# An MLP on scaled f16 pairs in place of fp32r pairs, with a range check and the old program behind it

## The chip, the core and the metric

The kernel runs on one core of a Trainium2 chip. The metric is device time in microseconds (us). TensorE (PE) multiplies matrices, VectorE (DVE) and ScalarE (ACT) work on elements, GpSimd (POOL) takes a few small things, SyncE (SP) issues the DMAs. The profile shows one execution, and its times count from the first instruction.

## The reference

```python
scores = (q @ k.T) / 8 + decay, causal            # 4 batches, 8 heads, 576 tokens, head size 64
x = softmax(scores) @ v                           # then as 2304 tokens x 512
h = x @ moe_w_in;   g = relu(h) ** 2;  x2 = g @ moe_w_out           # 512 -> 2048 -> 512
h = x2 @ moe2_w_in
g = where(h >= 1, h, where(h <= -1, 0, (h + 1) ** 2 / 4))
out = g @ moe2_w_out
```

q, k, v and f (from which the decay is a cumulated logarithm) are float32, the four weights float64. All but moe2_w_out are drawn eight times larger than the plain draw.

## The kernel before

The output is computed transposed, features on the partitions, tokens along the free dimension. The 2304 tokens are cut into four blocks: 0, 1 and 2 of 512 tokens, and a last one of 768. For every block attention comes first and then the two MLPs (`mo` 0 and 1). The attention of a later block is spread between the MLP steps of the blocks ahead of it, so all engines have two kinds of work at the same time.

Blocks 0 to 2 go through 96 steps (3 blocks x 2 MLPs x 16 feature chunks of 128). A step does 12 matmuls of 512 columns for the hidden part (`h_group`, L1122 to L1138) and 12 for the output part (`out_group`, L1170 to L1191). They are 12 because every operand is a pair of fp32r numbers, the value rounded and the rest: upper by upper, upper by rest, rest by upper. `act_group` (L1140) does the activation on ScalarE and VectorE and makes the pair `gh`, `gl` of the result; `finish` (L1193) makes the pair of x2 or writes the output.

The weights arrive as float64. `w_load` loads them, `decode` (L1041) makes fp32 out of the bits on ScalarE, VectorE and sometimes GpSimd, `w_split` (L1092) makes the pair. All of that happens while block 0 is worked on, 32 pairs of chunks in 32 steps. The pairs go to DRAM (`scr`), and every later step loads them from there.

The last block (`last_block`, L1300) works on quarters: 384 tokens by halves of the features, with the sums of a Strassen scheme that saves matmuls: `weight_sums` and `pair_sums` (L1236, L1272) make sums of weights, `token_sums` (L1311) of tokens. Matmuls there have 384 columns and lie in L1383, L1469 to L1471 and L1517. Per MLP there are eight pairs of chunks; nine of the sixteen have a hidden part of 42 matmuls (`seven`), seven one of 48, and all have 18 + 24 of the output part: 378 + 336 + 672 in sum.

The attention has its own matmuls: L701, L744 and L758 for the first 256 tokens of a sequence, L850, L851 and L957 for the rest.

`copies` (L622) rounds an operand to its upper part, on ScalarE (L626) or VectorE (L629); `subs` (L635) subtracts, on VectorE (L638); `add` (L1228) adds on VectorE (L1230). `top` (L643) is a masked minimum that also gives out an accumulated value.

The order of all of it is made on the host before the program is written: every operation has one or more engines with an estimated cost (`mm_t`, `act_t`, `dve_t` and the like), a due time, the operations it depends on and the buffers it holds. `Schedule.improve` tries several weights and due times with a model of the engines, keeps the shortest plan, and `emit` writes the instructions in that order. Every engine then runs its instructions in order. Which engine takes an operation with a choice, and which operation goes first, can thus change in all places when one cost changes. Buffers come from rings: `big` holds six buffers of 8 KB a partition for raw float64 weights and for pairs alike.

```python
def mm_t(n):
    return (n + 32) / 2400.0
```

Of the kernel before, what the change touches and what calls it, by code (L numbers as in the profile page):

```python
# [12 lines left out]
I32 = mybir.dt.int32  # L13
# [13 lines left out]
PS = 2.0 ** 15  # L27
LAG = 2
# [330 lines left out]
def mm_t(n):  # L359
    return (n + 32) / 2400.0  # L360
# [43 lines left out]
def tile_attention_moe_moe(ctx: ExitStack, tc: tile.TileContext, qkv, f, w2, outT):  # L404
    nc = tc.nc
    PSUM = bass.MemoryType.PSUM
# [54 lines left out]
    ring("sum", 2, [P, 2, 512], F32R, late=True)  # L461
    ring("ghl", 3, [P, 2, HALF], F32R, late=True)
    ring("xa", 1, [P, NKC, 2, 512], F32R)
    ring("xb", 1, [P, NKC, 2, WIDTH[LAST]], F32R)
# [26 lines left out]
    for s in range(NS):  # L491
        g, att = s // NFC, 0.0
        for blk, (g0, g1) in ATTENTION.items():
            if g0 <= g < g1:
                att += sum(pe_time(t) for t in [*tasks, *groups] if t.blk == blk) / (NFC * (g1 - g0))
        V.append(V[-1] + 24 * mm_t(nb(s)) + att)
# [29 lines left out]
    def setup():  # L526
        sb = new("xb", "setup", [P, 2 * NKC * WIDTH[LAST]], F32)
# [9 lines left out]
        sch.op(due + 90, {"POOL": (0.05, lambda: G.memset(half, 0.5))})  # L537
# [84 lines left out]
    def copies(out, in_, n, engines="ACT DVE POOL", psum=False):  # L622

        alts = {}
        if "ACT" in engines:
            alts["ACT"] = (act_t(n, psum), lambda: nc.scalar.activation(out(), in_(), AF.Copy))  # L626
        if "DVE" in engines:
            alts["DVE"] = (
                dve_t(n) if psum else dve2_t(n), lambda: nc.vector.tensor_copy(out(), in_()), *([] if psum else [True]))  # L629
# [5 lines left out]
    def subs(out, a, b, n, engines="DVE POOL"):  # L635
        alts = {}
        if "DVE" in engines:
            alts["DVE"] = (dve_t(n), lambda: nc.vector.tensor_sub(out(), a(), b()), True)  # L638
        if "POOL" in engines:
            alts["POOL"] = (pool2_t(n), lambda: nc.gpsimd.tensor_sub(out(), a(), b()))  # L640
        return alts
# [7 lines left out]
    def attention32(g):  # L649
# [67 lines left out]
        def recips(c, st, n, deps):  # L717
            def recip():
                nc.vector.tensor_scalar(st.tile[:, 1, :n], st.tile[:, 1, :n], 1e-9, None, op0=ALU.add)
                nc.vector.reciprocal(st.tile[:, 2, :n], st.tile[:, 1, :n])  # L720
# [31 lines left out]
        def products(c, got):  # L752
# [11 lines left out]
            for kcs in ([[0], [1]] if first else [[0, 1]]):  # L764
# [7 lines left out]
            xops.setdefault((g.blk, kc), []).append(sch.op(t0 + 5.5, {  # L772
                "DVE": (dve_t(HEAD), lambda kc=kc, hi=hi, av=av: nc.vector.tensor_tensor(
                    x.tile[:, kc, 1, g.off:g.off + HEAD], av.tile[:, :HEAD], hi().bitcast(F32), op=ALU.subtract))},
                [o3], [av, x]))
# [209 lines left out]
    def split_x(blk, kcs, off, src, n, deps, buf, due):  # L985

        x, unit, m = xb[blk], 1.0 / PS, n * len(kcs)
# [5 lines left out]
        o4 = sch.op(due + 0.5, {"DVE": (dve_t(m), lambda: nc.vector.scalar_tensor_tensor(  # L993
            lo(), src(), unit, hi().bitcast(F32), op0=ALU.mult, op1=ALU.subtract), True)}, [o3], [buf, x])
# [6 lines left out]
    scr = [dram.tile([P, 2, 2, 512], F32, name=f"scr{i}") for i in range(32)]  # L1001
# [5 lines left out]
    def w_load(s):  # L1007
# [10 lines left out]
        if first:  # L1018
            b = new("big", f"raw{s}", [P, 2, 512], U64) if W64 else new("wf", f"wf{s}")
# [12 lines left out]
        if again:  # L1032
            b = whl[s] = new("big", f"whl{s}")
            for pair, layers in again.items():
                c = span(layers)
                ops.append(sch.op(V0(s + 2) - 7, {
                    "SP": (dma_t(P * 4096 * len(layers), late=1.2), lambda b=b, c=c, pair=pair: nc.sync.dma_start(
                        out=b.tile[:, c].bitcast(F32), in_=scr[pair][:, c]))},
# [53 lines left out]
    def w_split(s):  # L1092
# [6 lines left out]
        if s not in whl:  # L1099
# [4 lines left out]
        src, unit = lambda: w.tile[:, c], 2.0 if W64 else 1.0  # L1104
# [4 lines left out]
        o = sch.op(due + 1, {"DVE": (dve_t(n), lambda: nc.vector.scalar_tensor_tensor(  # L1109
            lo(), src(), unit, hi().bitcast(F32), op0=ALU.mult, op1=ALU.subtract), True)}, [o], [w, b])  # L1110
        whl_op[s].append(o)
        for pair, layers in new_pairs[s].items():
            c_ = span(layers)
            store = sch.op(due + 6, {"SP": (dma_t(P * 4096 * len(layers)), lambda c_=c_, pair=pair: nc.sync.dma_start(
                out=scr[pair][:, c_], in_=b.tile[:, c_].bitcast(F32)))}, [o], [b])
# [6 lines left out]
    def h_group(s):  # L1122
# [6 lines left out]
        for kc in range(NKC):  # L1129
# [7 lines left out]
            o = sch.op(V[s] + 0.01 * kc, {"PE": (3 * mm_t(n), mms)}, [o, *whl_op[s - LAG], *deps], [ps, w, src], mlp=True)  # L1137
        h_op[s] = (ps, o)  # L1138

    def act_group(s):  # L1140
# [8 lines left out]
        if mo == 0:  # L1149
# [6 lines left out]
            o3 = sch.op(due + 0.5, {"ACT": (act_t(n), lambda: A.activation(gh.tile[:, :n], r.tile[:, :n], AF.Square))},  # L1156
                        [o1], [r, gh])
        else:
            o1 = sch.op(due, {"ACT": (act_t(n, True, 1), lambda: A.activation(  # L1159
                r.tile[:, :n], ps(), AF.Relu, scale=0.5, bias=half))}, [o], [psb, r])  # L1160
# [3 lines left out]
                g.tile[:, :n], r.tile[:, :n], 1.0, ps(), op0=ALU.min, op1=ALU.max))}, [o1], [psb, r, g])  # L1164
            o3 = sch.op(due + 0.5, copies(lambda: gh.tile[:, :n], lambda: g.tile[:, :n], n, "ACT DVE"), [o2], [g, gh])
        o4 = sch.op(due + 1, subs(
            lambda: gl.tile[:, :n], lambda: g.tile[:, :n], lambda: gh.tile[:, :n].bitcast(F32), n, "DVE"), [o2, o3], [g, gh, gl])
        gt[s] = (gh, gl, o3, o4)

    def out_group(s, when):  # L1170
# [4 lines left out]
        for d in range(NKC):  # L1175
# [14 lines left out]
            if fc == NFC - 1:  # L1190
                finish(blk, mo, d, a, n, when)  # L1191
# [552 lines left out]
```

## Time and profile before

| | |
|---|---|
| three runs | 916.62, 918.34, 918.52 us; median 918.34 |
| profiled execution, its span | 917.6 us (its time outside the span isn't given) |
| PE busy | 906.0 us, 99%, 4620 matmuls |
| DVE busy | 819.7 us, 89% |
| ACT busy | 693.4 us, 76% |
| POOL busy | 40.9 us, 4% |
| DMA | 264 MB by queue 1, 90.9% of 16 engines |
| granted clock of PE | 0.998 on the mean |

A busy share is an average over stages with different limits. Matmuls are pipelined: the time shown for one is longer than its distance from the next. A group of instructions is a line of code, an engine and a shape, with count, busy time and mean time of one, and behind the bar the idle time of the engine ahead of it and what ended it. The chain is the work that ended last, followed back from the end.

### The profile page before, as it was taken

The page shows a single profiled execution, that of the slowest core. Times are in us where ns is not written, and L with a number is a line of the kernel's source. Part 1 is how long each engine was busy: PE and PEld are TensorE (multiplying, and loading weights), DVE is VectorE, ACT ScalarE, POOL GpSimd, SP SyncE. Part 2 cuts the span into 40 slices and gives each one's busy share as a digit, 9 for nine tenths or more (in the row PEclk, how much of TensorE's full clock was granted, in tenths as well). Part 3 has the DMA queues.
Part 4 walks back from the last instruction along what each step waited for, and adds up shares of the span by engine and source line. Part 5 has one row for each costly group of instructions (what it writes and reads, how often), then busy time and mean ns, then how long its engine had stood idle before and what let it go on. Part 6 is the DMA issues. An engine that isn't in the chain of part 4 may idle for free.

```text
span 917.6 us, 14421 instructions
## 1 busy us (share of the span) xinstructions
PE 906.0 (99%) x4620; PEld 789.0 (86%) x4620; DVE 819.7 (89%) x1888; ACT 693.4 (76%) x1391; POOL 40.9 (4%) x134
## 2 busy tenths in 40 slices
PE   7999999999999999999999999999999999999998
PEld 6778788887888888888888888888899999999998
DVE  7999999999889889988788977999798997899994
ACT  6999889899878877987787787888674455566553
POOL 4101002220000000000000000000000000000000
PEclk9999999999999999999999999999999999999999
DMA  7899999898999997999999998998888988859782
GB/s 214 243 339 418 313 404 323 327 363 306 337 339 299 305 313 221 277 309 303 253 286 286 321 301 261 229 307 230 225 283 268 334 309 286 259 186 308 265 315 86
DMA packets 139835, 264.96 MB, mean 289 GB/s; under 512 B 91120, under 2 KB 95632, under 8 KB 124976
## 3 DMA queue, kind: packets, MB, share of 16 engines
q1 hardware_dynamic: 139752, 264.04, 90.9%
q8 instruction: 37, 0.61, 0.3%
q14 instruction: 38, 0.31, 0.1%
q10 hardware_dynamic: 8, 0.00, 0.0%
HBM read 186.22 MB, written 56.80 MB: 265 GB/s over the span
## 4 chain that ended last, share of the span: by engine, by line
PE 82%; DVE 9%; ACT 4%; DMA 2%; issue 2%; POOL 1%; DVEq 0%; ACTq 0%; POOLq 0%
PE h L1132 24%; PE acc L1183 8%; PE acc L1185 8%; PE acc L1184 8%; PE h L1517 6%; PE av L957 4%; PE X L1383 3%; PE Y L1383 2%; PE s L850 2%; PE s L851 2%; PE b L1469 2%; PE b L1470 2%; PE b L1471 2%; DMA PT<-PP 1%; PE c L1469 1%
## 5 line engine op out<-in xcount | busy, mean ns | idle before, releaser
L1132 PE MATMUL h<-x,whl 128*128 128x512 f32 x1128 | 283.1, 394 | 1.3 <-DVE whl L1109 0.7
L1132 PEld LDWEIGHTS h<-x,whl 128*128 128x128 f32 x1128 | 209.5, 188 | 45.2 <-DVE whl L1109 1.6
L1183 PE MATMUL acc<-gh,whl 128*128 128x512 f32 x384 | 150.8, 393 | 0.0
L1185 PE MATMUL acc<-gl,whl 128*128 128x512 f32 x384 | 150.3, 391 | 0.0
L1184 PE MATMUL acc<-gh,whl 128*128 128x512 f32 x384 | 149.9, 390 | 0.0
L1185 PEld LDWEIGHTS acc<-gl,whl 128*128 128x128 f32 x384 | 72.1, 188 | 15.6
L1183 PEld LDWEIGHTS acc<-gh,whl 128*128 128x128 f32 x384 | 72.1, 188 | 13.7 <-issue 0.5
L884 ACT ACTIVATE E<-E,st 128x448 f32<-128x448 f32 (+2 forms) x96 | 63.6, 663 | 26.6 <-DVE st L645 20.4
L1184 PEld LDWEIGHTS acc<-gh,whl 128*128 128x128 f32 x384 | 72.2, 188 | 13.4
L638 DVE TENSOR_TENSOR gl<-g,gh 128x512 fp32r<-128x512 f32 x96 | 68.6, 714 | 5.9 <-ACT gh L626 3.9
L926 DVE SCALAR_TENSOR_TENSOR PP<-E,st,PP 128x512 f16<-128x512 f32 (+2 forms) x128 | 70.3, 594 | 3.5 <-ACT PP L922 2.8
L922 ACT ACTIVATE PP<-E,st 128x512 f16<-128x512 f32 (+2 forms) x128 | 67.3, 590 | 4.7 <-DVE st L896 4.4
L645 DVE CUSTOM_DVE_ANT_0 E<-s,mask 128x288 f32<-128x288 f32 (+2 forms) x128 | 59.5, 498 | 6.2 <-PE s L851 5.7
L626 ACT ACTIVATE pr<-PT 128x640 fp32r<-128x640 f16 (+2 forms) x69 | 36.0, 571 | 16.7 <-DMA PT<-PP 16.5
L629 DVE CAST pr<-PT 128x640 fp32r<-128x640 f16 (+2 forms) x91 | 32.7, 408 | 16.2 <-DMA PT<-PP 16.0
L957 PE MATMUL av<-pr,vt 128*128 128x320 f32 (+2 forms) x288 | 44.4, 298 | 0.0
L957 PEld LDWEIGHTS av<-pr,vt 128*128 128x128 f32 x288 | 41.6, 189 | 2.9 <-issue 0.2
L1159 ACT ACTIVATE r<-h,half 128x512 f32<-128x512 f32 x48 | 32.5, 677 | 11.9 <-PE h L1132 11.6
L1163 DVE SCALAR_TENSOR_TENSOR g<-r,h 128x512 f32<-128x512 f32 x48 | 32.7, 682 | 8.6 <-ACT r L1161 7.7
L851 PE MATMUL s<-K,Q 128*128 128x288 f32 (+2 forms) x128 | 39.6, 317 | 0.0
L850 PE MATMUL s<-K,Q 128*128 128x288 f32 (+2 forms) x128 | 39.0, 316 | 0.1
L1053 ACT ACTIVATE wf<-raw 128x1024 f32<-128x1024 f32 (+1 forms) x31 | 34.5, 1114 | 6.0 <-DVE whl L1109 6.0
(390 smaller groups left out, 1993.9 us busy)
## 6 DMA issues: line engine op xcount, KB each, us to landing
whl<-scr SPq DMA_DIRECT2D x56, 1024.0 KB
raw<-in_w_dram SPq DMA_DIRECT2D x28, 1024.0 KB
scr<-whl SPq DMA_DIRECT2D x28, 1024.0 KB
wo<-scr SPq DMA_DIRECT2D x48, 512.0 KB
in<-in_qkv_dram SPq DMA_DIRECT2D x32, 608.0 KB
wi<-scr SPq DMA_DIRECT2D x23, 512.0 KB
si<-in_sum SPq DMA_DIRECT2D x18, 512.0 KB
whl<-scr SPq DMA_DIRECT2D x16, 512.0 KB
```

The lines of the kernel that those rows point to most:

```text
L638: alts["DVE"] = (dve_t(n), lambda: nc.vector.tensor_sub(out(), a(), b()), True)
L645: return nc.vector.tensor_tensor_reduce(out=out, in0=ps, in1=mask[:m, OFF - q0:OFF - q0 + n], scale=scale, scalar=3e38, op0=ALU.add, op1=A ...
L850: nc.tensor.matmul(out, q2[:, q0:q0 + m], k2[:, s0:s1], start=True, stop=False)
L851: nc.tensor.matmul(out, Q1.tile[:, q0:q0 + m], K1.tile[:, s0:s1], start=False, stop=True)
L884: nc.scalar.activation(Ec.tile[:m, :e], Ec.tile[:m, :e], AF.Exp, scale=-1.0, bias=nmx(), accum_out=st.tile[:m, 1, ci:ci + 1])))}, [*tops, ...
L922: nc.scalar.activation(hi, x, AF.Copy, scale=r())
L926: nc.vector.scalar_tensor_tensor(lo, x, r(), hi, op0=ALU.mult, op1=ALU.subtract)
L957: nc.tensor.matmul(av.tile[:, c0:W], vt.tile[:, kc, :, :], dst()[:, i, :], start=(j == 0), stop=(j == len(parts) - 1))
L1132: nc.tensor.matmul(ps.tile[:, :n], w.tile[:, 0, wi, kc * P:(kc + 1) * P], src.tile[:, kc, xi, :n], start=(kc == 0 and i == 0), stop=(kc == ...
L1183: nc.tensor.matmul(a.tile[:, :n], wh, gh.tile[:, :n], start=(fc == 0), stop=False)
L1184: nc.tensor.matmul(a.tile[:, :n], wl, gh.tile[:, :n], start=False, stop=False)
L1185: nc.tensor.matmul(a.tile[:, :n], wh, gl.tile[:, :n], start=False, stop=(fc == NFC - 1))
```

## The change

MLP operands become f16 pairs. Weights are multiplied by 2^10, x by 2^10, x2 by 2^2, the first activation by 2^4 and the second by 1, and the scales are taken out again where results leave PSUM. The attention keeps fp32r. The function is called twice with a new argument `halves`. In the call with `halves` on, every subtraction that makes a rest of weights, x, x2, weight sums or token sums, and every instruction that makes an output, also gives out its sum along the free dimension into a column of `seen`. `out_of_range` squares and sums these columns, compares six totals with limits, and the second call, the program of before on fp32r, stands in a conditional block that runs when one of them is outside. Scratch tensors in DRAM and rings get half the bytes; `big` has seven buffers and raw weights have a ring of three of their own. Some plain subtractions and additions become `scalar_tensor_tensor`, since a scale has to go in. The planner's cost of a matmul is changed for `halves`.

```diff
+SW, SX, SG = 2.0 ** 10, (2.0 ** 10, 2.0 ** 2), (2.0 ** 4, 1.0)
+SEEN = {"w": (48, 4.0, 1e30), "x": (64, 0.25, 1e30), "x2": (32, 0.25, 1e30), "s": (64, -1.0, 1e30), "t": (32, -1.0, 1e30),
+        "o": (32, 2.0 ** 16, 1e36)}
-def mm_t(n):
-    return (n + 32) / 2400.0
+def mm_t(n, halves=False):
+    return (n + (6 if halves else 32)) / 2400.0
...
+    T, TD, NB = (F16, F16, 2) if halves else (F32R, F32, 4)
+    sw, sx, sg = (SW, SX, SG) if halves else (1.0, (1.0, 1.0), (1.0, 1.0))
+    sh = [sw * x for x in sx]
...
-    ring("big", 6, [P, 2, 2, 512], F32R)
-    ring("gh", 3, [P, 512], F32R)
-    ring("gl", 2, [P, 512], F32R)
+    ring("big", 7 if halves else 6, [P, 2, 2, 512], T)
+    if halves:
+        ring("raw", 3, [P, 2, 512], U64, early=True)
+    ring("gh", 3, [P, 512], T)
+    ring("gl", 2, [P, 512], T)
...
+    def subs(out, a, b, n, engines="DVE", psum=False, scale=1.0, seen=None):
+
+        def run():
+            if scale == 1.0 and not seen:
+                nc.vector.tensor_sub(out(), a(), b())
+            else:
+                kw = {"accum_out": seen()} if seen else {}
+                nc.vector.scalar_tensor_tensor(out(), a(), scale, b(), op0=ALU.mult, op1=ALU.subtract, **kw)
+
+        return {"DVE": (dve_t(n) + (0.06 if seen else 0.0), run, *([] if psum else [True]))}
...
-        o = sch.op(due + 1, {"DVE": (dve_t(n), lambda: nc.vector.scalar_tensor_tensor(
-            lo(), src(), unit, hi().bitcast(F32), op0=ALU.mult, op1=ALU.subtract), True)}, [o], [w, b])
+        o = sch.op(due + 1, subs(lo, src, lambda: wide(hi()), n, scale=unit, seen=mark("w")), [o], [w, b])
...
+    def result_copy(out, src, n):
+        if not halves:
+            return copies(out, src, n, "ACT DVE", psum=True)
+        to = mark("o")
+        return {"ACT": (act_t(n, True) + 0.1, lambda: nc.scalar.activation(out(), src(), AF.Copy, scale=so[1], accum_out=to()))}
...
+            def plus_old(due, out, ps, old, deps, bufs, mo=mo, seen=None):
+                kw = lambda: {"accum_out": seen()} if seen else {}
+                return sch.op(due, {"DVE": (dve_t(n) + (0.06 if seen else 0.0), lambda: nc.vector.scalar_tensor_tensor(
+                    out(), ps(), so[mo], old(), op0=ALU.mult, op1=ALU.add, **kw()))}, deps, bufs)
...
+def out_of_range(ctx: ExitStack, tc: tile.TileContext, seen, marks):
...
+    v.memset(one, 1.0)
+    for i, (kind, (m, lo, hi)) in enumerate(SEEN.items()):
+        x = seen[kind][:, :marks[kind]]
+        v.scalar_tensor_tensor(x, x, 1.0, x, op0=ALU.mult, op1=ALU.mult, accum_out=sq[:, i:i + 1])
+        v.memset(lims[:, i, 0:1], lo)
+        v.memset(lims[:, i, 1:2], hi)
+    nc.sync.dma_start(out=lim, in_=lims)
+    total, count = ps.tile([n, 1], F32, name="total"), ps.tile([1, 1], F32, name="count")
+    nc.tensor.matmul(total, sq, one, start=True, stop=True)
+    v.tensor_tensor(ok[:, 0:1], total, lim[:, 0:1], op=ALU.is_ge)
+    v.tensor_tensor(ok[:, 1:2], total, lim[:, 1:2], op=ALU.is_le)
+    v.tensor_tensor(ok[:, 0:1], ok[:, 0:1], ok[:, 1:2], op=ALU.mult)
+    nc.tensor.matmul(count, ok[:, 0:1], one[:n], start=True, stop=True)
+    v.tensor_scalar(bad, count, n - 0.5, None, op0=ALU.is_lt)
+    return nc.values_load(bad[0:1, 0:1], min_val=0, max_val=1)
...
-        tile_attention_moe_moe(tc, *args, outT)
+        with tc.tile_pool(name="seen", bufs=1) as pool:
+            seen = {kind: pool.tile([P, m], _mybir.dt.float32, name=f"seen_{kind}") for kind, (m, _, _) in SEEN.items()}
+            marks = tile_attention_moe_moe(tc, *args, outT, True, seen)
+            bad = out_of_range(tc, seen, marks)
+        with tc.If(bad > 0):
+            tile_attention_moe_moe(tc, *args, outT, False, None)
```

## Rows read from the trace of the kernel before

**Rows 1.** The page, part 1: busy us of each engine, share, instructions.
```profile
PE 906.0 (99%) x4620; PEld 789.0 (86%) x4620; DVE 819.7 (89%) x1888; ACT 693.4 (76%) x1391; POOL 40.9 (4%) x134
```
**Rows 2.** Stretches: from:to, length, busy us (count) by engine, PEclk, DMA, GB/s.
```profile
40.00:222.00 182.00, 181.21 (x859) 146.28 (x858) 173.84 (x303) 164.53 (x277) 19.85 (x14) 1.00 0.95 353
222.00:663.00 441.00, 440.26 (x2134) 371.53 (x2133) 386.03 (x978) 354.50 (x737) 8.76 (x91) 1.00 0.99 284
...
700.00:866.00 166.00, 165.13 (x939) 162.03 (x938) 153.42 (x319) 95.38 (x188) 0.00 (x0) 1.00 0.82 278
```
**Rows 3.** The chain that ended last: shares by engine, then two pieces (start, us, what).
```profile
PE 82%; DVE 9%; ACT 4%; DMA 2%; issue 2%; POOL 1%; DVEq 0%; ACTq 0%; POOLq 0%
...
596.27 2.72 PE h L1132 x12
...
793.73 7.80 PE h L1517 x45
```
**Rows 4.** Stretches again, of L1132 on PE (two rows) and of L1184 (two rows).
```profile
40.00:222.00 182.00, 91.77 (x361) 1.00 0.95 353
222.00:663.00 441.00, 195.25 (x785) 1.00 0.99 284
...
40.00:222.00 182.00, 43.68 (x112) 1.00 0.95 353
222.00:663.00 441.00, 102.70 (x264) 1.00 0.99 284
```
**Rows 5.** Groups by shape on VectorE: busy us, mean ns, idle time ahead and its end.
```profile
L926 DVE SCALAR_TENSOR_TENSOR PP<-E,st,PP 64x384 f16<-64x384 f32 x32 | 19.5, 608 | 2.6 <-ACT PP L922 2.0
L638 DVE TENSOR_TENSOR ghl<-G,ghl 128x384 fp32r<-128x384 f32 x32 | 17.7, 553 | 0.9 <-ACT ghl L626 0.2
L894 DVE TENSOR_SCALAR st<-st 128x3 f32<-128x3 f32 x32 | 5.4, 168 | 4.8 <-ACT E L884 4.0
L645 DVE DVE_READ_ACCUMULATOR2_ANT mm<- 128x1 f32 x64 | 5.2, 81 | 0.0
L814 DVE TENSOR_SCALAR Q<-in 64x320 fp32r<-64x320 f32 x10 | 3.1, 311 | 1.5 <-DMA in<-in_qkv_dram 1.5
L736 DVE TENSOR_SCALAR E1q<-E1q,st1q 128x256 f32<-128x256 f32 x4 | 1.3, 346 | 0.0
L736 DVE TENSOR_SCALAR E1q<-E1q,st1q 128x128 f32<-128x128 f32 x4 | 1.1, 280 | 0.0
```
**Rows 6.** Stretches again, of L629 on VectorE, the last block.
```profile
663.00:917.60 254.60, 9.39 (x26) 1.00 0.77 262
```
**Rows 7.** Groups by shape on ScalarE.
```profile
L922 ACT ACTIVATE PP<-E,st 128x512 f16<-128x512 f32 x64 | 42.6, 708 | 0.0
L1159 ACT ACTIVATE r<-h,half 128x512 f32<-128x512 f32 x48 | 32.5, 677 | 11.9 <-PE h L1132 11.6
L1156 ACT ACTIVATE gh<-r 128x512 fp32r<-128x512 f32 x48 | 29.7, 619 | 0.0
L1150 ACT ACTIVATE r<-h 128x512 f32<-128x512 f32 x48 | 28.1, 586 | 4.5 <-PE h L1132 4.4
L884 ACT ACTIVATION_READ_ACCUMULATOR E<-E,st 128x1 f32 x64 | 12.0, 187 | 0.0
```
**Rows 8.** The page, parts 3 and 6: DMA queues, and the largest group of issues.
```profile
q1 hardware_dynamic: 139752, 264.04, 90.9%
q8 instruction: 37, 0.61, 0.3%
...
whl<-scr SPq DMA_DIRECT2D x56, 1024.0 KB
```
**Rows 9.** Order of time: the end, SP's wait there, a small memset.
```profile
913.50 1.08 DVE L1230 TENSOR_TENSOR p<-b,p 128x384 f32<-128x384 f32 x2 [4.12 <-PE b L1471]
914.09 0.86 SPq L1599 DMA_DIRECT2D out_dram<-p  x2
...
SPq L1733 <- DMA out_dram<-p: 1.6, 1, 1.6
...
0.73 0.10 POOL L533 MEMSET warm<- 128x1 f32 x1 [0.29 <-POOLq L1726]
```

More of the change, by code (lines that the diff above doesn't have):

```diff
@@ L620, in tile_attention_moe_moe, with copies @@
     pair, used = {}, []
-    def copies(out, in_, n, engines="ACT DVE POOL", psum=False):
+    def copies(out, in_, n, engines="ACT DVE POOL", psum=False, scale=1.0):
         alts = {}
         if "ACT" in engines:
-            alts["ACT"] = (act_t(n, psum), lambda: nc.scalar.activation(out(), in_(), AF.Copy))
+            alts["ACT"] = (act_t(n, psum), lambda: nc.scalar.activation(out(), in_(), AF.Copy, scale=scale))
         if "DVE" in engines:
-            alts["DVE"] = (
-                dve_t(n) if psum else dve2_t(n), lambda: nc.vector.tensor_copy(out(), in_()), *([] if psum else [True]))
+            alts["DVE"] = (dve_t(n) if psum else dve2_t(n), lambda: (
+                nc.vector.tensor_copy(out(), in_()) if scale == 1.0 else
+                nc.vector.tensor_scalar(out(), in_(), scale, None, op0=ALU.mult)), *([] if psum else [True]))
         if "POOL" in engines:
@@ L1018, in w_load @@
         if first:
-            b = new("big", f"raw{s}", [P, 2, 512], U64) if W64 else new("wf", f"wf{s}")
+            b = new("raw" if halves else "big", f"raw{s}", [P, 2, 512], U64) if W64 else new("wf", f"wf{s}")
             loads = []
@@ L1231, in add, with narrow @@
         return sch.op(due, alts, deps, bufs, slack)
-    scr2 = [dram.tile([P, 2, 512], F32, name=f"sum{i}") for i in range(2 * NPAIR)]
+    scr2 = [dram.tile([P, 2, 512], TD, name=f"sum{i}") for i in range(2 * NPAIR)]
     sum_op = {}
+    def narrow(b):
+        return b.tile.rearrange("p a n -> p (a n)").bitcast(T)[:, :1024].rearrange("p (a n) -> p a n", a=2)
     def weight_sums(i, due, W, o_w):
@@ L1313, in token_sums @@
             ta = new("xa", f"t{mo}_last", [P, 2 * NKC * 512])
-            rest = [new("o", f"t{mo}_o{i}") for i in range(4)] + [new("g", f"t{mo}_g{i}") for i in range(2)]
+            rest = [new(x, f"t{mo}_{x}{i}", [P, 512], T) for x, m in (("o", 4), ("g", 2)) for i in range(m)]
             def unit(t, kk, i):
@@ L1412, in squared @@
                 def squared():
-                    A.activation(rt(), src(), AF.Relu, scale=0.5, bias=half)
+                    A.activation(rt(), src(), AF.Relu, scale=0.5 / sh[1] ** 0.5, bias=half)
                     A.activation(rt(), rt(), AF.Square)
@@ L1540, in last_block @@
                         og[j, k] = sch.op(t0 + t_h + 0.5, {"DVE": (dve_t(n), lambda out=out, rt=rt, pst=pst: (
[L1541 removed]
+                            v.scalar_tensor_tensor(out(), rt(), sh[1], pst(), op0=ALU.min, op1=ALU.max)))},
                             [o1], [ps, r, gb])
@@ L1618, in last_block @@
                     part = scr4[mo, c][:, :, 2:].rearrange("p t a n -> p t (a n)") if done else scr2[mo * NPAIR + c]
-                    o_l = load(t0 - 7, lambda part=part: part, lambda sb=sb, j=j: sb.tile[:, j].rearrange("p t a n -> p t (a n)").bitcast(F32),
-                               P * 4096, out_sum_op[mo, c] if done else [sum_op[mo * NPAIR + c]], [sb])
+                    o_l = load(t0 - 7, lambda part=part: part, lambda sb=sb, j=j: wide(sb.tile[:, j].rearrange("p t a n -> p t (a n)")),
+                               P * 1024 * NB, out_sum_op[mo, c] if done else [sum_op[mo * NPAIR + c]], [sb])
                     for z, key, slot, dep, e in ((1, "c", 3, "b22", 0), (0, "b", 1, "t3", 1)):
```

210 lines of the change are left out of this document (112 added, 98 removed).

## The prediction

> **What bounds the kernel now.** I read the busy shares first: TensorE 99%, VectorE 89%, ScalarE 76% [rows 1]. A busy share alone proves nothing for a pipelined engine, so the second view is the chain that ended last: 82% of the span is TensorE [rows 3], and its pieces are long runs of matmuls with no gap between them. The third view is the table by stage [rows 2]. I cut the span where the work changes: 40 to 222 us is token block 0 with the decoding of the weights, 222 to 663 blocks 1 and 2 with the rest of the attention, and from 663 on the last block (700 to 866 is its dense part). TensorE is busy 181.2 of 182 us, 440.3 of 441 and 165.1 of 166, at a granted clock of 1.00, the 2.4 GHz level. So TensorE's rate of matmuls sets the time, and VectorE stands close behind: 173.8 of 182 us in the first stage (96%), 386.0 of 441 (88%) in the second, 153.4 of 166 (92%) in the dense last part. ScalarE has 90%, 80% and 57% there. A gain on TensorE therefore meets VectorE soon, and the first stage, where ScalarE is full too, meets it first.
>
> **What one matmul costs.** The duration of a single matmul (some 390 ns for 512 columns) includes the pipeline; what counts is the distance of one from the next. Two runs in the chain give it: 12 matmuls of 512 columns take 2.72 us, 226.7 ns each, and 45 of 384 columns take 7.80 us, 173.3 ns each [rows 3]. The difference of 128 columns is 53.4 ns, 0.417 ns a column, one column a cycle at 2.4 GHz. Taken off, 512 columns leave 226.7 - 213.3 = 13.3 ns and 384 leave 173.3 - 160.0 = 13.3 ns: a fixed part of each fp32r matmul.
>
> **Part 1: the f16 operands on TensorE.** The three products of a pair (upper by upper, upper by rest, rest by upper) stay three, so the number of matmuls doesn't change. What can go is the fixed part. The trace of before has no f16 matmul. Bounds: 0 ns (all of the 13.3 ns stays) and 13.3 ns (only the columns are left). A loss is excluded as far as the column rate goes, since that is already one a cycle and the operands only become narrower. I take 10.8 ns: the planner's formula in the diff replaces (n + 32)/2400 by (n + 6)/2400, and its old constant is just the 13.3 ns of the rows; that the new one is as good is an assumption. The Trainium skill (TensorE: Matmul & The Clock Gate, section Back-to-back issue gap) gives 2.5 ns over the columns at the high clock and names no type. The rows disagree for fp32r, with their 13.3 ns [rows 3], and nothing here shows f16. Carried over from the rows the saving would be nothing (rival b), by the rule 10.8 ns a matmul.
>
> How many: 2304 of 512 columns (96 steps of 24; the trace has 361 + 785 of L1132, and 112 + 264 of L1184, one of three such lines, in the first two stages [rows 4]) and 1386 of 384 columns in the last block (336 of L1517, 378 of L1383, 672 of L1469 to L1471, counted from the loops; 939 of them lie in 700 to 866 us [rows 2]). 3690 x 10.8 ns = 40.0 us if nothing else binds. By stage: (361 + 3 x 112) x 10.8 = 7.5 us; (785 + 3 x 264) x 10.8 = 17.0 us; the rest, 15.3 us, from 663 us on, 10.1 of it in 700 to 866.
>
> **Part 2: what VectorE and ScalarE pay.** The range sums ride on the instruction that makes the rest operand. An accumulated output shows in the trace as an instruction of its own, 81 ns on VectorE [rows 5] and 187 on ScalarE [rows 7]. Sums, from the loops: 32 for weights, 33 for x, 20 for x2, 40 for Strassen sums of weights, 16 of tokens, 6 results on VectorE: 147 x 0.08 = 11.8 us; 14 results on ScalarE, 2.6 us, spread thin. By stage VectorE gets about 41, 47 and 59: 3.3, 3.8 and 4.7 us.
>
> Many subtractions become scalar_tensor_tensor with an f16 operand and output. The only such row, L926 with 384 columns, takes 608 ns against 553 for a plain fp32r subtraction of as many (L638) [rows 5]: 55 ns more, which on some 350 instructions would be 19 us. But L926 reads its factor per partition, and such a factor alone costs L736 68 ns over L814 with a constant: L814's 311 ns at 320 columns are 278 at 256, by the 0.52 ns a column between L736's two widths, against L736's 346 [rows 5]. On ScalarE the f16 output of L922 takes 708 ns against 619 of L1156, +89, and a per-partition operand with f32 output (L1159 against L1150) +91 [rows 7]. So the factor explains it all, and f16 itself I take at 0, bounds 0 and 19 us on VectorE. Scales in activations and copies are constants and cost nothing by the same rows.
>
> First stage: VectorE 173.8 + 3.3 = 177.1 us against the 182 - 7.5 = 174.5 that TensorE would allow. The planner has to move work (the decode's masks, upper parts) to ScalarE with its 164.5 us; both together have 341.7 us for two engines, 170.8 each if perfectly shared. At 96% that is 178 us: I take 4 of the 7.5 us (bounds 0 and 7.5). Second stage: 386.0 + 3.8 = 389.8 of 424 us, 92%, ScalarE 84%: I take 15 of 17. Last part: in 700 to 866 VectorE would need 153.4 + 3.5 = 156.9 us against 155.9. But 26 casts, 9.4 us, run on VectorE from 663 us on [rows 6] while ScalarE is half idle, and the planner may give them away: I take 13 of 15.3. Sum 4 + 15 + 13 = 32 us.
>
> **Part 3: DMA and buffers.** The weight pairs' traffic halves (170 of the 264 MB become 85; the largest part are 56 loads of 1 MB, now half of it). The queue is 90.9% busy [rows 8], but only 2% of the chain is DMA [rows 3], so the gain is mostly cover for part 1: the weights have to come faster by the same 4%, and they will. The seven buffers and three separate ones for raw weights let the first loads start earlier; I take 0 to -3 us, at 0.
>
> **Part 4: the verdict at the end.** Nothing hides it: it needs the last result. Now the last VectorE addition ends at 914.58, its output's issue at 914.95, SP waits 1.6 us for the landing, and barriers, 1.0 us, end the span at 917.6 [rows 9]. After: two accumulator reads 0.2; 13 memsets at 0.10 and 6 squarings at 0.17 + 0.08 [rows 5, 9], 2.8, so 917.6; the limits' small DMA, 2.1 as the last output takes from issue to landing, 919.7; three comparisons 0.5, a matmul and its turn-round 0.3, one comparison 0.2, 920.7. Then all engines load the verdict and branch over the second program. No row shows either. Lower bound nothing; upper bound a DMA's 2.1 us for the load and, for the branch, a fetch of code: the queue of instructions spends 0.3% of 16 x 917.6 us on 37 packets, 1.2 us each [rows 8], which with a round trip of 2.1 makes 3.3, and two barriers of 1.0 beside. I take 1 + 3, nearer to the rows of a fetch, and 1.0 for the last barrier: 925.7, so +8. Bounds: with load and branch at nothing and the memsets done early +3, with all of it +12. The queue of instructions shows code arriving in packets, with no branch in it. The Trainium skill (Runtime: NRT & Kernel Launch, section Instruction fetch mechanics) says that a taken branch out of the window that was fetched ahead stalls for a fetch; it speaks against the change. With the fetch it would be the sum below, by a branch without one 3 us less.
>
> **Sum.** 917.6 - 32 + 8 = 893.6 us of span. The span of the profiled execution is 917.6 and the median of the three runs 918.34, so 0.7 us lie around it: **894 us**.
>
> **The rivals.** (a) *VectorE takes over.* If the planner can't move work and VectorE nowhere exceeds the 95.5% it has in the first stage, that stage takes 177.1/0.955 = 185.4 (a loss of 3.4), the dense last part 156.9/0.955 = 164.3 (1.7 gained), the second 15 and the rest of the last block 4: 17.3 gained, and with the verdict's 8 it is 909 us. For it: the first stage is at 96% and 90% on both engines; against it: casts that can go to an idle ScalarE. Were f16 to cost the 55 ns too, it would be 915 or more. (b) *The fixed part stays* (it is TensorE's turn from one set of weights to the next and not the width of fp32r): nothing is gained, the sums push VectorE to 97% in the first stage, some 2 us, and the verdict's 8 come on top: 918.3 + 2 + 8 = 928 us, slower. The point from which it decides: with four fifths of the saving used, 8 us need 8/(0.8 x 3690) = 2.7 ns a matmul. Against it: the same 13.3 ns at both widths looks like a cost of the weights' format. (c) *The second program runs.* Then it is 894 + about 915, some 1810 us. I worked the values out from the reference's inputs: scaled weights reach 1998, x 3391, the first activation 8618, x2 6822, the second 10585, all under f16's 65504, and the squared rests sum to 13262, 547 and 449 where 4, 0.25 and 0.25 are asked. So it should not. (d) *TensorE gets all of it*, VectorE's work being rearranged: 917.6 + 0.7 - 40 + 8 = 886, down to 877 with 13.3 ns.
>
> **Chances.** Forecast with its own surroundings (890 to 902) 0.48; (d) 0.20; (a) 0.19; (b) 0.09; (c) 0.02; the verdict far above its bounds or a planner's poor order, time near or above 918, 0.02. The range leaves out (b), (c) and the outer edge of (d): 880 to 914 us. 0.2% of 918 is 1.8 us, about what a measurement tells from no change. Of (a) a small part ends within that: faster 0.85, same 0.03, slower 0.12.
>
> **What would show it.** Right: runs of 512-column matmuls at 216 ns and of 384 at 162.5; VectorE at 95% or more between 40 us and the end of block 0, with accumulator reads of 80 ns; TensorE with its first real gaps there; some 180 MB moved; an end of 8 us more after the last addition, most of it without work. Wrong: matmuls still 226.7 ns apart; f16 subtractions longer than 553 ns at 384 columns; TensorE idle more than 10 us in the second stage; a tail over 12 us longer; or a span of twice the length.

## The result and the profile after

The changed kernel takes 886.24 us (median of 4 runs, 885.75 to 888.5), the kernel before 917.85 us beside it: ratio 0.966, interval [0.965, 0.968], 31.6 us less. The profiled execution spans 883.8 us. The second program did not run. Of the forecast, 894 us with 880 to 914 around it, the range held; the point was 8 us too high, and rival (d), 886 us, is what came, its number in part by luck (see the sum below). Two executions are left out of the medians below, one of 1280 us with the engines held, at a granted clock of 0.66, and one of 2322 us of the kernel before.

The page of the changed kernel, parts 1, 3 and 4 (busy us, share and count by engine; the large queue's packets, MB and share; the chain's shares), against [rows 1, 3, 8]:

```profile
PE 862.5 (98%) x4624; PEld 476.8 (54%) x4624; DVE 819.6 (93%) x2067; ACT 688.9 (78%) x1413; POOL 26.4 (3%) x128
...
q1 hardware_dynamic: 139764, 175.04, 66.5%
...
PE 62%; DVE 22%; ACT 8%; issue 4%; POOL 1%; DMA 1%; SPq 0%; DVEq 0%; ACTq 0%; POOLq 0%
```

TensorE's busy time fell by 43.5 us at as many matmuls (the four more are the verdict's). VectorE's is the same to 0.1 us, though it has 179 more instructions. TensorE is still 62% of the chain, VectorE now 22% instead of 9%: it has come close behind.

The changed kernel's chain in order of time (start, us, what), two runs of matmuls of 512 and 384 columns, against [rows 3]:

```profile
606.46 2.59 PE h L1153 x12
...
651.81 5.36 PE h L1554 x33
```

2.59/12 is 215.8 ns and 5.36/33 is 162.4 ns. Less the columns (213.3 and 160.0) 2.5 and 2.4 ns are left, where fp32r had 13.3. The saving per matmul is 10.9 ns, against 10.8 predicted.

The table by stretch (from:to, length, busy us and count by engine, granted clock, DMA share, GB/s), cut where the counts of matmuls answer to the cuts of [rows 2]:

```profile
40.00:215.00 175.00, 173.53 (x866) 84.64 (x863) 171.91 (x344) 167.05 (x281) 2.81 (x5) 1.00 0.82 275
215.00:638.00 423.00, 421.42 (x2128) 228.36 (x2127) 390.42 (x1027) 345.86 (x737) 10.63 (x93) 1.00 0.73 199
638.00:829.00 191.00, 187.56 (x1140) 111.47 (x1139) 180.56 (x428) 117.67 (x239) 0.00 (x0) 1.00 0.47 149
```

Matmul by matmul, the end of the first stage comes 7 us earlier than before, that of the second 25 us, the dense part's end (866 us before) 37 us, and the last addition, whose end was at 914.58 [rows 9], comes at 875.5: 39.0 us earlier. Some 2 of these 39.0 us seem to belong to the execution that was profiled and not to the change: it spans 917.6 us, while the 34 other executions of the kernel before whose span is on record take 914.7 to 917.1, and its granted clock was 0.83 between 10 and 20 us (in part at the lower level, 1.2 GHz), where the changed kernel has 1.00. By the medians 31.6 us plus the 5.3 us of a longer end (below), 36.9 of the predicted 40.0 us, arrived. The first stage got its share, less up to 2 us of that kind, with VectorE at 98% and ScalarE at 95%.

The end of the changed kernel, VectorE in order of time (start, us, operation, idle time ahead), and rows of the branch's line (count, ns shortest/median/longest, first and last start):

```profile
874.97 0.56 DVE L1602 SCALAR_TENSOR_TENSOR p<-b,p 128x384 f32<-128x384 f32 x1
875.45 0.08 DVE L1602 DVE_READ_ACCUMULATOR p<-b,p 128x1 f32 x1
...
876.87 0.15 DVE L1752 TENSOR_SCALAR bad<-count 1x1 int32<-1x1 f32 x1 [0.28 <-PE count L1751]
...
L1810 ACTq COMPARE_BRANCH  x1: 50/50/50, 877.7 to 877.7; - x1
...
L1810 PEldq COMPARE_BRANCH  x1: 3678/3678/3678, 877.8 to 877.8; - x1
...
L1810 SPq COMPARE_BRANCH  x1: 58/58/58, 878.0 to 878.0; - x1
...
L1810 ACTq EVENT_SEMAPHORE  x1: 17/17/17, 881.4 to 881.4; - x1
...
L1810 SPq EVENT_SEMAPHORE  x8: 17/17/17, 881.9 to 882.4; - x8
```

The verdict is there at 877.02, 1.5 us after the last addition. Five of the six squarings, the memsets and the limits' DMA ran earlier. Then all engines load the verdict and branch. ScalarE's branch takes 50 ns and TensorE's 3678 ns in its row, until 881.5. But ScalarE's next instruction starts only at 881.4, 3.7 us after its branch and before TensorE's has ended, and SyncE's at 881.9, 3.8 us after its own; VectorE's (881.8) comes 3.8 us after too, GpSimd's alone 0.5 us after. So four engines stand still for the same time, each by itself, and the end doesn't hang on TensorE: SyncE, the last, goes through eight short instructions on semaphores and a barrier until the span ends at 883.8. From the last addition it is 8.3 us, 3.0 before: 5.3 more, where I had 8. So 39.0 - 5.3 = 33.7, and 917.6 - 883.8 is 33.8; the 31.6 us of the medians are the better figure, for the reason given above.

Four questions were left for experiments: what the end costs, why VectorE took nothing, whether the planner had to do anything for it, and what the halved traffic is worth.

### The profile page after: what moved, and what is told of

Read it like the earlier page. It is cut to its first block, busy times and chain, and to the rows that moved or that the text cites. A ratio compares the mean times of both kernels' runs of the same rounds, so it can differ in the third digit from the quotient of the medians.

```text
span 883.8 us, 14535 instructions
## 1 busy us (share of the span) xinstructions
PE 862.5 (98%) x4624; PEld 476.8 (54%) x4624; DVE 819.6 (93%) x2067; ACT 688.9 (78%) x1413; POOL 26.4 (3%) x128
## 4 chain that ended last, share of the span: by engine, by line
PE 62%; DVE 22%; ACT 8%; issue 4%; POOL 1%; DMA 1%; SPq 0%; DVEq 0%; ACTq 0%; POOLq 0%
PE h L1153 17%; PE acc L1205 6%; PE acc L1207 6%; PE acc L1206 6%; PE av L980 4%; PE h L1554 4%; PE X L1419 3%; DVE whl L663 2%; PE Y L1419 2%; PE s L873 2%; PE s L874 2%; DVE wf L1095 2%; DVE gl L663 2%; PE b L1506 1%; PE b L1508 1%
## 5 line engine op out<-in xcount | busy, mean ns | idle before, releaser
L1153 PE MATMUL h<-x,whl 128*128 128x512 f16 x1128 | 266.6, 380 | 0.8 <-DVE g L1185 0.5
L1153 PEld LDWEIGHTS <-whl 128*128 128x128 f16 x1128 | 106.5, 98 | 129.8 <-issue 5.1
L1205 PE MATMUL acc<-gh,whl 128*128 128x512 f16 x384 | 146.2, 381 | 1.4 <-ACT o L1221 1.4
L1206 PE MATMUL acc<-gh,whl 128*128 128x512 f16 x384 | 145.7, 379 | 0.0
L1207 PE MATMUL acc<-gl,whl 128*128 128x512 f16 x384 | 145.6, 379 | 0.0
L907 ACT ACTIVATE E<-E,st 64x320 f32<-64x320 f32 (+2 forms) x96 | 63.5, 662 | 38.9 <-DVE st L669 25.7
L663 DVE SCALAR_TENSOR_TENSOR gl<-g,gh 128x512 f16<-128x512 f32 x96 | 65.7, 684 | 5.9 <-ACT gh L1177 3.2
L1207 PEld LDWEIGHTS <-whl 128*128 128x128 f16 x384 | 37.6, 98 | 45.1
L1205 PEld LDWEIGHTS <-whl 128*128 128x128 f16 x384 | 37.5, 98 | 44.3 <-issue 3.7
L1206 PEld LDWEIGHTS <-whl 128*128 128x128 f16 x384 | 37.7, 98 | 39.7 <-issue 1.4
L873 PE MATMUL s<-K,Q 128*128 128x288 f32 (+2 forms) x128 | 51.0, 410 | 0.1
L980 PE MATMUL av<-pr,vt 128*128 128x320 f32 (+2 forms) x288 | 50.1, 318 | 0.0
L1554 PEld LDWEIGHTS <-wi 128*128 128x128 f16 x336 | 32.8, 98 | 22.8 <-issue 0.7
L874 PE MATMUL s<-K,Q 128*128 128x288 f32 (+2 forms) x128 | 39.5, 316 | 0.0
L663 DVE SCALAR_TENSOR_TENSOR whl<-wf,whl 128x1024 f16<-128x1024 f32 (+1 forms) x32 | 37.9, 1185 | 0.7 <-ACT whl L1128 0.6
L1075 ACT ACTIVATE wf<-raw 128x1024 f32<-128x1024 f32 (+1 forms) x31 | 34.8, 1124 | 3.1 <-DVE whl L663 2.4
```

What stands on the lines that cost most here:

```text
L663: nc.vector.scalar_tensor_tensor(out(), a(), scale, b(), op0=ALU.mult, op1=ALU.subtract, **kw)
L873: nc.tensor.matmul(out, q2[:, q0:q0 + m], k2[:, s0:s1], start=True, stop=False)
L907: nc.scalar.activation(Ec.tile[:m, :e], Ec.tile[:m, :e], AF.Exp, scale=-1.0, bias=nmx(), accum_out=st.tile[:m, 1, ci:ci + 1])))}, [*tops, ...
L980: nc.tensor.matmul(av.tile[:, c0:W], vt.tile[:, kc, :, :], dst()[:, i, :], start=(j == 0), stop=(j == len(parts) - 1))
L1153: nc.tensor.matmul(ps.tile[:, :n], w.tile[:, 0, wi, kc * P:(kc + 1) * P], src.tile[:, kc, xi, :n], start=(kc == 0 and i == 0), stop=(kc == ...
L1205: nc.tensor.matmul(a.tile[:, :n], wh, gh.tile[:, :n], start=(fc == 0), stop=False)
```

## What the end of the kernel costs

Four kernels take the test apart. Without load, branch and second program:

```diff
-    return nc.values_load(bad[0:1, 0:1], min_val=0, max_val=1)
+    return bad
...
-        with tc.If(bad > 0):
-            tile_attention_moe_moe(tc, *args, outT, False, None)
```

> The changed kernel with the range sums and the computed verdict, but without the load of the verdict, the branch and the second program: this part, which would run only for values out of range, is left out. Theory (the tail's price is the load and TensorE's fetch behind the branch): the load's 0.5 us, TensorE's 3.7 us and the barrier between them go, 881.5 to 882.5 us against 886.2 of the changed kernel. Rival (the tail is paid by the verdict's own chain of sums, or the time lies in the body): 885 us or more.

Measured: 881.07 us (880.95 to 881.16). Without the sums and the verdict as well:

```diff
     def mark(kind):
-        if not halves:
-            return None
+        return None
         i = marks[kind] = marks.get(kind, 0) + 1
...
-        to = mark("o")
+        return copies(out, src, n, "ACT DVE", psum=True, scale=so[1] if halves else 1.0)
...
-            bad = out_of_range(tc, seen, marks)
```

(The results' copies so have a choice of engine again.)

> The f16 pairs alone: no range sums, no verdict, no branch, no second program (all of the range test is left out). Theory (TensorE sets the time, VectorE's 11.8 us of accumulator reads lie beside it): only the verdict's 1.5 us go beside what the run without the branch saves, 880 to 881 us. Rival (VectorE binds together with TensorE, as in rival a): another 5 to 8 us go, 873 to 876 us.

Measured: 881.02 us (880.87 to 882.6), the same. All the arithmetic of the range test is free in a kernel without the branch. The 1.5 us of the verdict that I expected back had cost nothing there: the last output's DMA lands after the verdict is known (at 877.4 us; SyncE goes on at 878.0), as SyncE's waits in the run without the branch show (line, what it waits for: us, times, longest).

```profile
SPq L1805 <- DMA out_dram<-p: 1.7, 1, 1.7
```

With load and branch, but a body of one instruction:

```diff
-        with tc.If(bad > 0):
-            tile_attention_moe_moe(tc, *args, outT, False, None)
+            with tc.If(bad > 0):
+                nc.vector.memset(seen["o"], 0.0)
```

> The changed kernel with load and branch, but with a single memset as the body of the branch in place of the second program (which is left out). Theory (TensorE's 3.7 us at the branch are a fetch of code from far away): with the target a few instructions on, TensorE's branch takes under 0.1 us like those of the other engines, 882.5 us. Rival (the branch itself costs TensorE 3.7 us, wherever it leads): 886 us.

Measured: 882.16 us (882.06 to 883.07). The last one leaves the whole body, but lets the usual case fall through:

```diff
-        with tc.If(bad > 0):
+        with tc.If(bad > 0, preferred_fallthrough_block=False):
```

> The changed kernel, nothing left out, but the second program is placed behind the end as the branch's target, so that the usual case falls through. Theory (a taken branch to code that is not there costs the fetch): TensorE's branch takes under 0.1 us, 882.5 us, which would beat the changed kernel by 3.5 us. Rival (the branch itself costs it, or the engine drops what it fetched ahead at any conditional branch): 886 us.

Measured: 886.79 us (885.91 to 889.18), no gain. TensorE's and ScalarE's rows of the branch's line and a queue of instructions (packets, MB, share), of the short body and then of the fall-through (the changed kernel's queue has the same line):

```profile
L1810 PEldq COMPARE_BRANCH  x1: 223/223/223, 878.5 to 878.5; - x1
...
q14 instruction: 39, 0.32, 0.1%
...
L1810 ACTq COMPARE_BRANCH  x2: 38/38/39, 879.3 to 879.4; - x2
...
L1810 PEldq COMPARE_BRANCH  x2: 95/1914/3733, 879.4 to 879.7; - x2
L1810 ACTq EVENT_SEMAPHORE  x1: 17/17/17, 879.4 to 879.4; - x1
...
q14 instruction: 46, 0.38, 0.1%
```

With a near target TensorE's branch takes 223 ns, more than the 0.1 us expected but not 3.7. In the fall-through version there are two branches: the condition takes 95 ns, but then a second jump leads over the body to the end, and that one takes 3733. So it is the far target that costs, not the condition. The other engines agree: with the near target ScalarE goes on 0.2 us after its branch (878.4 to 878.6); in the fall-through its next instruction comes within 0.1 us of the condition, but 2.9 us after the jump (879.4 to 882.3). And code is fetched in that time: in the changed kernel five packets of the queues of instructions start between 878.6 and 879.1 us, in the run with the short body none between 858.1 and 881.2, and the page counts seven more on this queue. By medians: load and near branch, beyond the output's landing beside them, 882.16 - 881.07 = 1.1 us, the far target 886.24 - 882.16 = 4.1 us, of which some 3.5 are the stop (3.7 less 0.2) and some 0.6 SyncE's eight semaphore instructions, which the short body doesn't have; the sums and the verdict 0, though with the branch the verdict's 1.5 us stand ahead of the load. The Trainium skill (Runtime: NRT & Kernel Launch, Instruction fetch mechanics) says that a taken branch out of what was fetched ahead stalls for a fetch; TensorE's 3678 ns against 223 ns to a near target agree, and so do the five packets.

## Why VectorE took nothing

I had charged 147 reads of the accumulator at 81 ns. The time that counts is the distance from one instruction's start to the next one's. VectorE in order of time, 1024 columns to f16, first with a sum (changed kernel), then without one (run without the sums):

```profile
299.12 1.22 DVE L663 SCALAR_TENSOR_TENSOR wfi<-si,shi 128x1024 f16<-128x1024 f32 x1
300.26 0.08 DVE L663 DVE_READ_ACCUMULATOR wfi<-si,shi 128x1 f32 x1
300.26 0.47 DVE L669 CUSTOM_DVE_ANT_0 E<-s,mask 64x320 f32<-64x320 f32 x1
...
51.24 1.22 DVE L662 SCALAR_TENSOR_TENSOR whl<-wf,whl 128x1024 f16<-128x1024 f32 x1
52.38 0.69 DVE L1091 TENSOR_SCALAR wf<-wf 128x1024 int32<-128x1024 int32 x1
```

Either way the next instruction starts 1.14 us after the subtraction: 300.26 - 299.12 and 52.38 - 51.24. The read starts while the subtraction's last 0.08 us still run, and takes no time of its own. The kernel before showed it already, in a kind of read that it had:

```profile
57.79 0.28 DVE L645 CUSTOM_DVE_ANT_0 E4q<-s4q,mask 128x128 f32<-128x128 f32 x1
58.00 0.08 DVE L645 DVE_READ_ACCUMULATOR2_ANT st4q<- 128x1 f32 x1
58.01 1.23 DVE L1073 CUSTOM_DVE_ANT_0 wf<-wf,low 128x2048 uint16<-128x2048 uint16 x1
```

The next instruction there starts 0.01 us after the read. The price of f16 in the subtraction was rightly put at 0: 384 columns take 552 ns after (`L663`) against 553 before [rows 5].

How much more would VectorE have borne? Two kernels without the branch put a memset ahead of each subtraction with a scale or a sum, unknown to the planner (351 of them; 1 column, then 96):

```diff
+                nc.vector.memset(marks_extra, 0.0)
                 kw = {"accum_out": seen()} if seen else {}
                 nc.vector.scalar_tensor_tensor(out(), a(), scale, b(), op0=ALU.mult, op1=ALU.subtract, **kw)
```

> The run without the branch (load, branch and second program left out) with a tiny memset on VectorE ahead of each of its some 350 subtractions with a scale or a sum, which the planner doesn't know of: some 60 ns each, 20 us in all, the upper bound that the prediction gave for f16. Theory (as the run without the sums shows, VectorE's busy share has slack in it): 0 to 5 us more than 881.1. Rival a (VectorE binds beside TensorE): 12 to 20 us more, 893 to 901 us.

> As the run before, with a memset of 96 columns, some 0.15 us each, 50 us in all: VectorE would be busy for 870 of 879 us. It must bind now by either theory; the question is from where on. If the slack in it was 15 us or so: 915 us. If all of its load lies on the path: 930 us. If TensorE still hides most: under 900 us.

Measured: 883.27 us (882.86 to 886.69) and 887.56 us (887.36 to 890.13). The second kernel's added group and page (busy us, mean ns; busy us by engine):

```profile
L663 DVE MEMSET seen_extra<- 128x96 f32 x351 | 48.4, 138 | 1.3
...
PE 867.5 (98%) x4624; PEld 479.0 (54%) x4624; DVE 837.4 (94%) x2418; ACT 690.0 (78%) x1413; POOL 26.6 (3%) x128
```

The 48.4 us of memsets make VectorE busy for 17.3 us more, not 48 (837.4 against 820.1 in the run without the branch), since they overlap with their neighbours too; the 20.7 us of the first kernel made 3.7 (823.8). So my "20 us" and "50 us" weren't added as meant, and the question of 20 real us can't be read from the first. In busy time: 3.7 us cost 2.2 us, and 17.3 us cost 6.5 (against 881.07). Of the first some two fifths stay hidden, of the second three fifths; the first cost is no larger than the spread of the runs (882.86 to 886.69). VectorE is near the bound, but not beside TensorE in it, as rival (a) had it.

## Whether the planner had to do anything

Three kernels separate the rate from the plan. The first two have the f16 pairs without the branch, once with the old cost of a matmul, once with every operation that has a choice of engine held to the engine of the kernel before (a table of engines read into the planner):

```diff
-    return (n + (6 if halves else 32)) / 2400.0
+    return (n + 32) / 2400.0
```

> The run without the branch (load, branch and second program are left out, as there; 881.1 us), with the planner told the old cost of a matmul, (n + 32)/2400, for the f16 products too. Theory (TensorE's own rate makes the gain, and the plan only has to keep it fed): within 3 us of 881. Rival (the gain needs a plan made for the faster matmuls): 889 us or more.

Measured: 891.31 us (890.53 to 892.0), the rival's value: 10.2 us of the gain (against 881.07) need a plan that knows the new rate.

```diff
+        for o, k in zip(self.ops, was):
+            keep = [x for x in o.alts if x[0] == k]
+            if keep:
+                o.alts = {x: o.alts[x] for x in keep}
```

> The run without the branch (load, branch and second program left out), with each operation that has a choice of engine kept on the engine that it had in the kernel before. Rival a as predicted (the planner must move work away from VectorE or VectorE takes over): 890 to 905 us. Theory from the run without sums (VectorE has slack even where it is 98% busy): 881 to 885 us.

Measured: 890.76 us (890.7 to 893.73); the ratio's interval against before is [0.969, 0.973]. 9.7 us are lost: on the rival's side, if barely, and less than the 22.7 us (40 less 17.3) that it had priced. Where it goes stands in the first stretch of the table and in one wait of TensorE (line, what it waits for: us, times, longest), both of the execution of 893.73 us:

```profile
40.00:215.00 175.00, 165.81 (x810) 80.41 (x810) 167.98 (x329) 156.17 (x267) 19.37 (x13) 0.99 0.80 264
...
PE h L1209 <- DVE whl L719: 6.0, 6, 1.8
```

By 215 us it is some 60 matmuls behind, 12 us, and all of the loss is there; up to 3 of the 12 are this execution's own, whose granted clock was 0.83 between 10 and 20 and between 205 and 215 us. GpSimd has 19.4 us of work where the changed kernel has 2.8 (the parts of the decode that were its own before), VectorE is at 96%, and TensorE waits for weight pairs. So the first stage is as tight as I had said; but the planner had a way out that I hadn't looked at, taking the decode's pieces from GpSimd (2.38 us each) to VectorE (1.22 us each). That these pieces make the loss is read from the rows; no run moves them alone. The other side of the test is the fp32r program alone with the new cost:

```diff
-        V.append(V[-1] + 24 * mm_t(nb(s), halves) + att)
+        V.append(V[-1] + 24 * mm_t(nb(s), True) + att)
...
-            marks = tile_attention_moe_moe(tc, *args, outT, True, seen)
...
-            tile_attention_moe_moe(tc, *args, outT, False, None)
+        tile_attention_moe_moe(tc, *args, outT, False, None)
```

(and every other `mm_t(..., halves)` of the products called with True.)

> The fp32r program alone (no f16 pairs, no range test, no branch), with the planner told the new cost (n + 6)/2400: the plan changes, the operands don't. Theory (the rate of the f16 matmuls makes the gain): no gain, 917 to 923 us. Rival (a better order of work makes it): under 905 us.

Measured: 920.68 us (918.34 to 922.3), ratio 1.003, interval [1.002, 1.004]. A plan for faster matmuls without faster matmuls gains nothing.

## What the halved traffic is worth

Two kernels without the branch put a copy within DRAM beside each transfer that the f16 pairs halved, in SyncE's queue. In the first each copy is as large as the transfer; in the second it moves one row and not 128, and everything else is the same:

```diff
+        sch.op(due, {"SP": (dma_t(size, late=1.2), lambda: nc.sync.dma_start(out=junk[i % 16][:, :c], in_=w2[i % 32][:, :c]))}, deps)
```

The second's line in its place:

```diff
+        sch.op(due, {"SP": (dma_t(size, late=1.2), lambda: nc.sync.dma_start(out=junk[i % 16][:1, :c], in_=w2[i % 32][:1, :c]))}, deps)
```

> The run without the branch (load, branch and second program left out), with a copy within the chip's memory of the same size beside each transfer that the f16 pairs halved, so that about 85 MB of traffic come back, issued from the same queue. Prediction (traffic is hidden, part 3 at 0): within 1.5 us of 881. Rival (the 30 us for which ScalarE and VectorE waited for the transposed rows by DMA in the kernel before come back and reach TensorE): 884 to 892 us.

> The run with the traffic given back, with the same program, plan and order of the queue, but each of the 262 copies moves one row of at most 4 KB and not 128: the issues stay, the traffic goes (load, branch and second program are left out, as there). Theory (the 35 us of that run are the traffic): 881 to 886 us. Rival (the issues in SyncE's queue and the changed plan cost them): 905 us or more.

Measured: 916.48 us (911.58 to 922.27) with the traffic, 881.7 us (880.71 to 884.82) with the issues alone. The bytes cost 34.8 us, more than either theory had, and nearly the whole gain; the issues cost nothing. The large queue, the chain's shares, two stretches and the waits for the transposed rows, with the traffic and then with the issues alone:

```profile
q1 hardware_dynamic: 177492, 264.05, 92.6%
...
DVE 39%; PE 24%; DMA 17%; ACT 12%; issue 5%; SPq 2%; DVEq 0%; ACTq 0%
...
215.00:638.00 423.00, 413.19 (x2061) 221.11 (x2060) 373.07 (x993) 344.63 (x733) 9.06 (x91) 1.00 1.01 292
638.00:829.00 191.00, 176.87 (x1010) 101.27 (x1009) 159.05 (x380) 109.19 (x223) 0.00 (x0) 0.96 0.88 277
...
DVE pr L649 <- DMA PT<-PP: 25.2, 13, 4.8
ACT pr L646 <- DMA PT<-PP: 23.3, 14, 5.1
```

```profile
q1 hardware_dynamic: 148148, 175.75, 68.0%
...
PE 67%; DVE 19%; ACT 8%; issue 3%; DMA 3%; SPq 0%; ACTq 0%; DVEq 0%
...
215.00:638.00 423.00, 422.34 (x2140) 229.74 (x2139) 384.52 (x1020) 355.28 (x753) 9.30 (x91) 1.00 0.74 199
638.00:829.00 191.00, 188.10 (x1136) 110.82 (x1134) 180.97 (x429) 119.87 (x243) 0.00 (x0) 1.00 0.48 153
...
DVE pr L649 <- DMA PT<-PP: 6.4, 6, 1.7
ACT pr L646 <- DMA PT<-PP: 2.5, 4, 1.0
```

With the traffic the DMA share is 1.01 in the second stretch. There TensorE falls 79 matmuls behind, in the third another 126, and VectorE and ScalarE wait 48.5 us for DMA transposes that come late, 8.9 with the issues alone. The last transpose is issued at 650 us; behind it both wait for the last block's own transfers (19.5 us in all for weights, their sums and output). In the third stretch the clock is 0.96 too, where TensorE has gaps, and 1.00 with the issues alone: at most 7.6 us (0.04 x 191) of the 34.8 lie in that. The copies are a rough stand-in: the queue's packets take 92.6% of 914.8 us, 847 us, against 90.9% of 917.6, 834 us, before, and a copy writes to DRAM where most of the real transfers went to SBUF. So the 35 us are what this DMA time costs, 13 us of packets more than before, with copies that stand ahead of real transfers in the queue; that the real transfers at their old size would cost just as much isn't shown.

## What one matmul pays beside its columns

The last kernel has bare matmuls only, 24 or 48 to a section. Its sections follow each other as 512 columns in fp32r and f16, 384 in fp32r and f16, 512 with weights of 64 columns in fp32r and f16, bf16, 256 in fp32r and f16, and then fp32r with the same weights each time.

> Bare matmuls alone, nothing of the reference is computed (the output is zeros): rows of 24 or 48 back to back for each type and width, on lines of their own. Theory (the 13.3 ns of an fp32r matmul and the 2.5 ns of an f16 one are fixed parts of the type, whatever the width): 226.7 ns at 512 and 173.3 at 384 and 120 at 256 columns for fp32r, 215.8, 162.5 and 109.2 for f16, bf16 as f16; and 226.7 again for fp32r with the same weights, or with weights of 64 columns. Rival (the fixed part is the load of the weights showing through, 188 against 98 ns a load): with weights of 64 columns fp32r falls to about 220 ns or less, with 256 columns a matmul takes 188 ns or more.

Its chain in order of time (start, us, what):

```profile
19.61 5.49 PE k L140 x24
25.10 5.20 PE k L142 x24
30.30 4.17 PE k L144 x24
34.47 3.92 PE k L146 x24
38.39 5.54 PE k L148 x24
43.93 5.30 PE k L150 x24
49.22 5.29 PE k L152 x24
54.51 5.75 PE k L154 x48
60.26 5.26 PE k L156 x48
65.52 5.47 PE k L158 x24
...
L154 PEld LDWEIGHTS k<-mr,wr 128*128 128x128 f32 x48 | 5.9, 192 | 0.1
```

By section: fp32r 228.8, 173.8 and 119.8 ns at 512, 384 and 256 columns, f16 216.7, 163.3 and 109.6, each a few ns too long at most for the change of section (226.7 and 215.8 inside the kernels). The fixed part is about 13 and about 3 ns at every width. Weights of 64 columns don't lower it (230.8 in fp32r), nor does loading the same weights again and again (227.9). At 256 columns a load of weights takes 192 ns (the last row) and a matmul comes every 119.8: loads overlap one another and don't show through. So the fixed part goes with the type, as Part 1 took it, and rival (b)'s reading is out.

## Why the prediction was right, and by how much not

- *What bounds the kernel.* TensorE's rate, right. But the kernel before stood at a second bound that I read past: DMA, with a share of 0.99 of 441 us in the second stage [rows 2]. That is 437 us of packets where a TensorE at f16's pace leaves 423. No run has the halved traffic with fp32r's matmuls, so what it is worth alone isn't measured; TensorE, busy for 440.3 of those 441 us, leaves it little.
- *Part 1.* 10.8 ns a matmul, 40.0 us: measured 10.9 ns, and 36.9 us by the medians (39.0 by the last addition of the profiles). The 10.8 was taken over from the diff's own formula and not from a row, so its fit is that formula's. The Trainium skill (TensorE: Matmul & The Clock Gate, Back-to-back issue gap) has N/2.4 + 2.5 ns for the gap of an isolated matmul, and for a stream of 512 columns 131 ns; f16's rows agree with the first (215.8 ns), fp32r's don't, and no row here comes near the second.
- *Part 2* held the mis-sized term. The discount for VectorE was 8 us (32 of 40); by stage I had 4, 15 and 13 us of gain, and by the profiles it was 7, 18 and 14, up to 2 us of the 7 being the profiled execution's own. Two steps failed in it. The 11.8 us of accumulator reads were counted by their duration, though for TensorE I had used the distance; by distance they are 0 to 0.01 us each, and leaving out all sums gains 0.05 us. And a busy share of 96% was taken as a ceiling, while it went to 98%. Right was that the planner had to rearrange: held to the old engines it loses 9.7 us, with the old cost 10.2.
- *Part 3.* Its own gain at 0 stands untested alone, but "only 2% of the chain is DMA" was a wrong reason to call it cover and pass on. Given back, the bytes cost 34.8 us. VectorE's and ScalarE's 32.5 us of waits for DMA transposes before (16.0 and 16.5) are 1.8 after.
- *Part 4.* +8, measured +5.3, within +3 to +12. "Nothing hides it" was wrong: the sums, memsets and limits' DMA ran early and the rest lies beside the last output's landing where no branch hangs on it. Load and near branch were 1.1 us, the far target 4.1, where I had 1 + 3 and a barrier of 1.0.
- *The sum.* 918.3 - 32 + 8 = 894.3 was forecast; by the medians it is 917.85 - 36.9 + 5.3 = 886.2. Of the 8.1 us, 4.9 are Part 2 (32 against 36.9), 2.7 Part 4 and 0.5 the start. The 0.7 us "around the span" compared two executions: taken on one, time and span lie 1.8 us apart before and 1.95 after (885.75 and 883.8).
- *Rivals.* (d) nearly came true in its mechanism (36.9 of 40), but that its 886 is right to 0.3 us is luck: its 40 us are 3.1 too many and its 8 us 2.7 too many, and the two cancel. (a) has its condition, a planner that can't move work, in the run with the engines held, at 891 us, some 896 with the branch's 5.2, and not 909. (b) and (c) didn't happen.

The one other version that keeps the second program, the fall-through, doesn't beat the changed kernel; the 881 us without a branch are what a kernel without that safety would take.

## What to carry to other kernels

Price every added instruction by the distance between starts, on each engine alike: a read that runs beside its neighbour's last 0.08 us costs nothing, whatever its own duration. Before taking a gain on the engine that bounds, compare every other resource's busy time in each stage with the shorter stage: DMA at 99% was a bound that the chain of waits showed only once the first one moved (2% of the chain before, 17% in the run with the traffic). Before believing a small difference between two profiles, compare each with the other executions of its kernel. A jump over a long program has its price whichever way the condition falls, as long as some jump leads over it.

## What I had not expected of the hardware

- A taken branch over the second program stops four engines for 3.7 to 3.8 us each, and TensorE 0.2 us with a target close by. Only TensorE's row shows it; the others' branches last 50 to 72 ns, and the stop is the gap to their next instruction.
- A memset of 96 columns (138 ns) ahead of a subtraction lengthens VectorE's busy time by 49 ns (17.3 us / 351), one of a single column (59 ns) by 11.
- Loads of fp32r weights of 192 ns go on behind matmuls that come every 120 ns.
